# Cluster attention and a softplus feed-forward layer on one core: another table of the issue order behind the first 900 of 3,790 steps, with the engine choices that go with it

## The chip, the cores and the metric

The kernel runs on one core of a Trainium2 chip. The metric is the device time of one execution in microseconds. Its engines are TensorE (PE in the rows; PEld is its weight load), VectorE (DVE), ScalarE (ACT), GpSimd (POOL) and SyncE (SP), which issues the DMAs. Each engine works through its own list in order; an instruction whose input isn't ready holds all that stand behind it on that engine.

## The reference

Four batches of eight heads, 768 positions of 64 elements. Queries and keys are assigned to the nearest of 16 centroids of their head, and a query attends only to keys of its own cluster. The result, as 3,072 rows of 512, goes through two dense layers with a softplus between.

```
q_assign = argmax(q_n . c_n);  k_assign = argmax(k_n . c_n)
scores = q @ k.T / 8, -1e9 where q_assign != k_assign
attn = exp(scores - max) / sum;  x = attn @ v
h = x @ w_in                      # 3072x512 @ 512x2048
g = max(h, 0) + log1p(exp(-|h|))
out = g @ w_out                   # 2048x512
```

## The kernel before, in words

**Attention.** There are 192 tiles, each of 128 queries of one head against that head's 768 keys. For tiles 30 and up `scores` emits four score matmuls (line 1104, 384 columns each), the negated row maximum on VectorE (1120), exp on ScalarE (1131), the cast of the result to an fp16 high part on ScalarE or GpSimd (311, names `phl`), and the low part, a subtraction, on GpSimd or VectorE (1147). A DMA transposition (333, `pt<-phl`) turns both halves, and `attend` multiplies them with the values (1196 to 1198, 18 short matmuls). The scores have two PSUM banks (ring `s`), so a tile's matmuls wait for the exp of the tile two before it.

**First layer.** A pass is 384 tokens of all heads; there are eight. `ffn1` computes a hidden group of 128 columns with twelve matmuls (1275 to 1277), because each fp32 operand is split into two fp16 halves and three of their four products are kept. The hidden groups use two banks (ring `h`). `softplus` follows: exp (1510), log (1511), and a VectorE operation (1526) that frees the bank; then a cast (311, `gh`) and a subtraction (1551). In passes 2 to 6, three of the eight pairs of hidden groups are computed by `seven_of` with seven half-size products in place of eight: three runs of 18, 12 and 12 matmuls (1451 to 1453), with VectorE additions (1462, 1483) and a copy (538) between them. Sums of activations (`tforms`, tile `tf`) and of weights (`wforms`, tiles `wf`, `wg`) are made on VectorE, GpSimd and ScalarE, and the weight sums sit in one buffer each of `pt`, `phl` and `p32` until `give_back`.

**Second layer.** `ffn2` (1895 to 1897, 512 columns) uses one bank (ring `o`); the last two passes use seven products for a whole 2x2 block (1772 to 1774).

**What sets the order.** Every stage is a generator that yields one operation at a time. `Order.run` reads `PLAN`, a string of two-character numbers; each number says which generator emits its next operation. So `PLAN` alone sets the order on all five engines. `either` and `cast` hold two engines for an operation; a key in `SWAPPED` takes the second one. `FILL` puts small matmuls of no use (292) ahead of some of the first matmul operations.

Of the kernel before, what the change touches and what calls it, by code (L numbers as in the profile page):

```python
# [41 lines left out]
SWAPPED = ('S1h_0', 'S1h_2', 'S1l_0', 'S2_2', 'S2_3', 'S2h_2', 'S2h_3', 'S2l_0', 'S2l_2', 'S2l_3', 'S3h_3', 'S3l_1', 'S3l_3', 'S4_0', 'S4_2', 'S4h_0', 'S4h_2', 'S4h_3', 'S4l_0', 'S4l_3', 'T1a_0', 'T1a_1', 'T1a_2', 'T1b_1', 'T1b_2', 'T1h_0', 'T1l_0', 'T1l_2', 'T2a_0', 'T2c_3', 'T2h_0', 'T2h_1', 'T2h_2', 'T2h_3', 'T2l_2', 'T3a_0', 'T3a_1', 'T3a_2', 'T3a_3', 'T3b_1', 'T3c_1', 'T3c_3', 'T3h_0', 'T3h_3', 'T3l_1', 'T4a_0', 'T4a_1', 'T4a_2', 'T4c_0', 'T4c_1', 'T4l_2', 'T4l_3', 'g0_1', 'g0_2', 'g0_4', 'g0_5', 'g0_7', 'g1_1', 'g1_3', 'g1_4', 'g1_6', 'g1_7', 'g2_3', 'g2_7', 'g3_1', 'g3_3', 'g4_0', 'g5_3', 'g5_4', 'g5_5', 'g5_7', 'g6_2', 'g6_3', 'g6_4', 'g6_6', 'g7_4', 'g7_7', 'gh0_0', 'gh0_4', 'gh0_6', 'gh2_2', 'gh2_4', 'gh3_0', 'gh3_1', 'gh3_2', 'gh4_2', 'gh4_4', 'gh4_5', 'gh4_7', 'gh5_1', 'gh5_3', 'gh5_4', 'gh5_6', 'gh6_0', 'gh6_1', 'gh6_2', 'gh6_4', 'gh6_5', 'gh6_6', 'gh6_7', 'gh7_4', 'gh7_5', 'k0_1', 'k10', 'k16', 'k20', 'k24', 'k8', 'kT1_0_1', 'kT1_2_0', 'kh10', 'kh16', 'kh2', 'kh22', 'kh4', 'kh6', 'm0_0_0', 'm0_0_1', 'm0_1_0', 'm20_4_0', 'm20_5_0', 'm28_6_0', 'm4_0_1', 'm8_2_0', 'p108', 'p110', 'p112', 'p114', 'p115', 'p119', 'p121', 'p124', 'p125', 'p127', 'p129', 'p136', 'p137', 'p143', 'p147', 'p151', 'p157', 'p16', 'p161', 'p163', 'p165', 'p169', 'p170', 'p172', 'p173', 'p174', 'p175', 'p176', 'p177', 'p179', 'p18', 'p187', 'p188', 'p189', 'p19', 'p191', 'p21', 'p22', 'p23', 'p26', 'p28', 'p29', 'p32', 'p34', 'p35', 'p37', 'p38', 'p41', 'p46', 'p48', 'p50', 'p51', 'p53', 'p57', 'p59', 'p64', 'p72', 'p75', 'p77', 'p80', 'p81', 'p87', 'p88', 'p93', 'p96', 'p97', 'p98', 'ph103', 'ph104', 'ph105', 'ph106', 'ph107', 'ph108', 'ph110', 'ph111', 'ph112', 'ph113', 'ph114', 'ph115', 'ph117', 'ph120', 'ph125', 'ph130', 'ph132', 'ph133', 'ph135', 'ph137', 'ph140', 'ph141', 'ph153', 'ph154', 'ph155', 'ph156', 'ph159', 'ph163', 'ph164', 'ph165', 'ph177', 'ph179', 'ph181', 'ph187', 'ph191', 'ph20', 'ph30', 'ph36', 'ph45', 'ph48', 'ph53', 'ph59', 'ph68', 'ph72', 'ph78', 'ph86', 'ph89', 'ph90', 'ph93', 'ph95', 'q0_0_0', 'qT0_0', 'qT1_1', 'tf2_1l', 'tf2_2a', 'tf2_2l', 'tf2_3h', 'tf2_4c', 'tf2_4h', 'tf3_1a', 'tf3_1b', 'tf3_1c', 'tf3_1h', 'tf3_1l', 'tf3_2a', 'tf3_2c', 'tf3_3c', 'tf3_3h', 'tf3_3l', 'tf3_4a', 'tf3_4c', 'tf3_4l', 'tf4_1a', 'tf4_2a', 'tf4_2l', 'tf4_3c', 'tf4_3l', 'tf5_1a', 'tf5_1b', 'tf5_1h', 'tf5_1l', 'tf5_2c', 'tf5_3l', 'tf5_4a', 'tf5_4c', 'tf6_1a', 'tf6_1c', 'tf6_1l', 'tf6_2a', 'tf6_2h', 'tf6_2l', 'tf6_3h', 'tf6_3l', 'tf6_4a', 'u10', 'u19', 'u20', 'u21', 'u22', 'u23', 'u27', 'u28', 'u2_3', 'u3_2', 'u3_3', 'u5_4', 'u6_4', 'v0', 'v14', 'v2', 'v2_2', 'v30', 'v3_4', 'v4', 'v5_4', 'v8', 'vh0', 'vh12', 'vh18', 'vh22', 'vh24', 'vh26', 'w17', 'w19', 'w20', 'w21', 'w22', 'w26', 'w27', 'w28', 'w30', 'wb1', 'wb10', 'wb11', 'wb12', 'wb13', 'wb14', 'wb15', 'wb16', 'wb17', 'wb18', 'wb19', 'wb2', 'wb20', 'wb21', 'wb22', 'wb23', 'wb24', 'wb25', 'wb27', 'wb28', 'wb29', 'wb3', 'wb31', 'wb4', 'wb5', 'wb6', 'wb7', 'wb8', 'wb9', 'wf2_1c', 'wf2_1h', 'wf2_2c', 'wf2_2h', 'wf2_2l', 'wf2_3c', 'wf2_3l', 'wf2_4a', 'wf2_4c', 'wf2_4l', 'wf3_1a', 'wf3_1b', 'wf3_1c', 'wf3_1l', 'wf3_2a', 'wf3_2c', 'wf3_3a', 'wf3_3b', 'wf3_3c', 'wf3_4l', 'wf4_1h', 'wf4_1l', 'wf4_2a', 'wf4_2l', 'wf4_3a', 'wf4_3b', 'wf4_3h', 'wf4_3l', 'wh0', 'wh1', 'wh11', 'wh12', 'wh13', 'wh16', 'wh18', 'wh21', 'wh23', 'wh24', 'wh25', 'wh27', 'wh28', 'wh29', 'wh3', 'wh30', 'wh4', 'wh5', 'wh6', 'wk2a', 'wk2b', 'wk2c', 'wk3a', 'wk3b', 'wk3c', 'wk4c', 'x2_0', 'x2_2', 'x3_2', 'x4_1', 'x4_2', 'x5_1', 'x6_1', 'x6_3', 'x7_1', 'xh1_2', 'xh1_3', 'xh2_0', 'xh2_1', 'xh3_0', 'xh3_3', 'xh4_3', 'xh5_2', 'xh6_0', 'xh6_1', 'xh6_3', 'xh7_0', 'xh7_3', 'zk0', 'zk10', 'zk12', 'zk14', 'zk16', 'zk2', 'zk22', 'zk24', 'zk26', 'zk30', 'zk4', 'zk6', 'zk8', 'zq0_0_0', 'zq0_0_1', 'zq12_3', 'zq16_5', 'zq20_5', 'zq24_7', 'zq28_7', 'zq4_0', 'zq4_1', 'zq8_2', 'zq8_3')  # L42
# [25 lines left out]
    "4h0lcz4d4f4f0ld44j4f4agb0ld44h4h4j4h4ld44jgbcz4hcz4l4j4cd44egb4e0o4f4e4l4n0l4nczd44hgcgc4pgc4l0o4e4jgdd44e4l"
    "0pd0cz4ggd4p0o4ncz4ngd4r4p4j4igd4l4rd44tczgd4n4k4t4p0pcz4r4v4pd44rgf4t4rgf0n4nged04p0p4x4vd4gg4t4xd44e4md00p"
    "d00p4v4z4oge4q4td44v4rgegf4zcz4xgf4t4x4q0p4q4v4q0p510pcz4zgf514s4v0p4x534x5153d7d04q554z4z4u51gh53g74w4q5355"  # L70
    "d70p0pghghgh51554zczd7czgi53d7d7gi515557590p57gi4y590p554qcz50d7gi520pd7530p52czgicz59575b52gj5bgj52d05dgk57"
    "0qcz0p5d55d70p54d7d0d7gl575759d74e59d7565bd05fd70q5bgjcz0q5f585d5b5dglgl5h5h595b5d5fczczglgmglgm5h5jgm5fcz5d"
    "5hdagngndadada5f0q5a5c5f525jda5j5h5l5lgn5ed052da5ng95e5j0q5e5lcz5p5h5n5ed0gn5jdacz5lda5l0q5e5g5p5j5i5nda5n0q"
    "gp5rgogngp5ngp5kcz5p5e0q0q0r5r5pcz5l5t5rdagq5n5p0q5t0q5t5m5t525vgqd00r5r0r5egq0qcz5r5vczczczgqda5p0qdade5vgr"
    "gq5o0q5xd0da5z5rd4degr5td4gsgggsd4de0q5x5vde5qdegsd0grgsdegr0rd05vgt0qcz5xd45tdede5xd0615vgs5z5qd40tdedecz0r"
    "d05x0ude61de0r61de5z0tgude5qd063ded0de5zde0r5zguded7d7655q5s5x0r61615ugudfgv65d0dfdf656363630td75q5z5wdf67df"
    "65df63d7df67695y616560670u69d06bd70s690udfgwgwgw62gx62gx676b63cz5q67656dcz0rgxd00r0v69gy676262gxd00v6dgy690s"
    "64gy6b6bgzdg0sgy6b690r0u6fdg6f666ddg6b6d6f6hdg6d68dggy6a6fdgdg6j6h6j6hdgh00rh0h00wd0h16ch1d0h1gxczh26f6hh1cz"
    "0vh2h1h3h3dah362czgv6l6dda6e0u0u0ucz0u6jh40u0r0yh4d00u6hczh40w0udadada0uh4czh60s6l6fh60u6l0w6nd0h60ydhh7dh6p"
    "6ldh6n62dhd06pdh6e6eh46jdh6jd06edh0ydhh8h80zh8h9h96ld0h55q6h6ph96n0w6gh56ncz0w0wczha6ihad06j0w0whbhacz0z0wcz"  # L80
    "cz0w6lha0w6n6phc6phchahc0w6e0zd0czhd6k6mhd0shed0626e0s6n0she6o0she6pgzczh9h90s0scz0z0shf0sd0hf6q0s0s0s0zhf0z"
    "6qd06q0z0x0s6ehe0zczcz0zhe6qhg0z6q6q6q6rdjhidjhi6td06r6rhiczdjdj6r6t6v0z0wdj6rczdj6thi6t6v6v6t6xd0dj6v10hjh7"
    "6x6vdj6z6xdjd06zd06r6t0zhkhj6x6s71d0hj6z0xd0djhidjdj6x716u736vdjdkdj6zdjd06zdk71717371djdjdk7375d06x75730x77"
    "djdkdkdk7775dk796zhm73d077dkhn106whn7b756y7975hnhoho79cz7d117311ho1111hlcz7b71hmd070hphphlhpdldlhpdld00zdldl"
    "d0hpdldldlhqhrhohrhrhsd0hshs117d1111cz7779hs77cz75791172d0hqhsho11ht0x72htht117bdm111111dm11d01172dm77dm727d"
    "74dmdmdmdm7d11hu767bhuhuhvhvhvd00x7bcz7978hw0x7d0x0xhv0x0x7b0x0xcz0x0xhx0x7dhxhx0xd07a72hxcz10hxhvczcz72czhy"
    "hyhy7f7hcz7c7f7f7f7h7h727h7jhz7fcz7l7j7l7h7f7ed07j7j7h7e7n7e7li07l7e7pd07j7j7ehz7e7n7nd07g7p7l7i7rhz7pi07n7p"
# [1896 lines left out]
```

## Time and profile before

| | us |
|---|---|
| timed runs: median of 3 | 852.97 |
| lowest and highest | 846.71, 854.46 |
| the profiled execution | 853.94 |
| its span in the trace | 852.2 |
| busy: TensorE, VectorE, ScalarE, GpSimd | 789.3, 693.8, 523.0, 598.4 |

The span runs from the first instruction to the last, and the profiled execution's own time is 1.7 us more. A busy engine is one with an instruction in flight. TensorE's matmuls overlap, and their ends are modelled: a 384-column matmul is shown as 0.33 us long, though the next one starts 0.16 us after it. So a gap between two matmuls that the trace calls idle is shorter than the time by which the second is late.

### The profile page before, as it was taken

The numbers are of one execution on the slowest core, as the hardware profiler recorded it, in microseconds if no ns is written. First come the engines' busy times: TensorE is split into PE (matmuls) and PEld (weight loads), VectorE is DVE, ScalarE is ACT, GpSimd is POOL, SyncE is SP. The second block draws the span as 40 slices with busy tenths as digits, with TensorE's granted clock in tenths as the row PEclk, the third lists the DMA queues.
The fourth block names the chain that finished last, engine by engine and source line by source line (L and its number), as shares of the span: only waits on it lengthen the run. The fifth ranks groups of instructions, "written<-read, shape, count | busy, mean of one in ns | idle before, by whom it ended". The sixth has DMA issues, their size and how long they took to land. (4 is left out here: it accounts for less than half of the span.)

```text
span 852.2 us, 20795 instructions
## 1 busy us (share of the span) xinstructions
PE 789.3 (93%) x8374; PEld 540.3 (63%) x8374; DVE 693.8 (81%) x1131; ACT 523.0 (61%) x846; POOL 598.4 (70%) x498
## 2 busy tenths in 40 slices
...
GB/s 311 242 254 157 101 189 250 204 209 205 199 197 196 186 154 184 141 181 105 154 121 196 189 197 169 201 182 166 141 157 184 155 136 94 59 113 23 33 1 56
DMA packets 402420, 136.15 MB, mean 160 GB/s; under 512 B 379028, under 2 KB 395924, under 8 KB 402324
## 3 DMA queue, kind: packets, MB, share of 16 engines
...
q14 instruction: 31, 0.25, 0.1%
...
## 5 line engine op out<-in xcount | busy, mean ns | idle before, releaser
L1147 POOL TENSOR_TENSOR phl<-p,phl 128x768 f16<-128x768 f32 x104 | 179.9, 1733 | 54.9 <-ACT phl L311 49.6
L1131 ACT ACTIVATE p<-s,negm 128x768 f32<-128x768 f32 x162 | 144.8, 896 | 86.9 <-DVE negm L1120 72.7
L1120 DVE TENSOR_REDUCE negm<-s 128x1 f32<-128x768 f32 x162 | 151.8, 948 | 16.3 <-PE s L1104 16.2
L1104 PE MATMUL s<-kt,qt 128*128 128x384 f16 x648 | 130.3, 325 | 8.8 <-ACT p L1131 6.5
L1275 PE MATMUL h<-xT,wi 128*128 128x384 f16 x392 | 128.4, 328 | 8.1 <-DVE fg L1526 6.0
L1276 PE MATMUL h<-xT,wi 128*128 128x384 f16 x392 | 128.4, 327 | 0.0
L1277 PE MATMUL h<-xT,wi 128*128 128x384 f16 x392 | 128.3, 327 | 0.0
L1196 PE MATMUL mbank<-vb,pt 128*128 128x65 f16 x1056 | 111.7, 192 | 7.6 <-DMA pt<-phl 5.1
L1198 PE MATMUL mbank<-vb,pt 128*128 128x65 f16 x1056 | 111.3, 194 | 0.9 <-DVE pt L1071 0.9
L1197 PE MATMUL mbank<-vb,pt 128*128 128x64 f16 x1056 | 111.6, 192 | 0.0
L1895 PE MATMUL o<-wo,gh 128*128 128x512 f16 x288 | 109.0, 379 | 2.3 <-DVE ot L1918 1.6
L1896 PE MATMUL o<-wo,gh 128*128 128x512 f16 x288 | 109.1, 379 | 0.1
L1897 PE MATMUL o<-wo,gh 128*128 128x512 f16 x288 | 109.1, 379 | 0.0
L1196 PEld LDWEIGHTS <-pt 128*128 128x128 f16 x1056 | 97.6, 98 | 18.0 <-DMA pt<-phl 9.0
L311 ACT CAST phl<-p 128x768 f16<-128x768 f32 x113 | 93.3, 829 | 25.3 <-DMA pt<-phl 20.7
L1197 PEld LDWEIGHTS <-pt 128*128 128x128 f16 x1056 | 97.2, 97 | 11.2 <-issue 2.7
L1198 PEld LDWEIGHTS <-pt 128*128 128x128 f16 x1056 | 97.3, 97 | 1.0 <-DVE pt L1071 1.0
L1510 ACT ACTIVATE fa<-h 128x384 f32<-128x384 f32 x98 | 47.8, 489 | 78.7 <-PE h L1277 74.6
L1104 PEld LDWEIGHTS <-qt 128*128 128x128 f16 x648 | 59.7, 97 | 49.0 <-issue 10.7
L1147 DVE TENSOR_TENSOR phl<-p,phl 128x768 f16<-128x768 f32 x58 | 67.8, 1171 | 7.4 <-POOL phl L311 4.0
L311 POOL CAST phl<-p 128x768 f16<-128x768 f32 x49 | 44.4, 909 | 28.7 <-ACT p L1131 17.7
L1511 ACT ACTIVATE fa<-fa 128x384 f32<-128x384 f32 x113 | 59.0, 523 | 2.3
...
## 6 DMA issues: line engine op xcount, KB each, us to landing
...
pt<-phl SPq DMA_TRANSPOSE x162, 4.0
...
```

What stands on the lines that cost most here:

```text
L311: (e.copy if e is nc.scalar else e.tensor_copy)(dst, src)
L1104: nc.tensor.matmul(st[:, j, :SH], qt[:, s, i], kt[:, s, NT // 2 * j : NT // 2 * (j + 1)], start=(s == 0), stop=(s == 1),)
L1120: yield op("DVE", 950, lambda: nc.vector.tensor_reduce(negm, st[:, :, :SH], AX.XY, ALU.max, negate=True))
L1131: yield op("ACT", 900, lambda: nc.scalar.activation(p32, st[:, :, :SH], AF.Exp, bias=negm, scale=size))
L1147: lambda e: e.tensor_tensor(phl[:, 1], p32, phl[:, 0], ALU.subtract),
L1196: nc.tensor.matmul(av, pt[:, 0, c], vb[:, c, D : 2 * D + 1], start=(c == 0), stop=False)
L1197: nc.tensor.matmul(av[:, :D], pt[:, 0, c], vb[:, c, :D], start=False, stop=False)
L1198: nc.tensor.matmul(av, pt[:, 1, c], vb[:, c, D : 2 * D + 1], start=False, stop=(c == NT - 1))
L1275: nc.tensor.matmul(hp, w[0], x[0], start=(c == 0), stop=False)
L1276: nc.tensor.matmul(hp, w[0], x[1], start=False, stop=False)
L1277: nc.tensor.matmul(hp, w[1], x[0], start=False, stop=(c == NP - 1))
L1896: nc.tensor.matmul(po, g[0], wo[:, f, 0, 1], start=False, stop=False)
```

## The change

Three tables of numbers change, and nothing else: `FILL`, `SWAPPED` and `PLAN`. `PLAN` keeps its first 900 entries and its length of 3,790. `SWAPPED` goes from 451 to 474 keys, of which 290 are the same. On GpSimd there are 22 more instructions, on ScalarE 17 fewer, on VectorE 5 fewer; TensorE has two more of the filling matmuls and otherwise the same ones; SyncE issues the same DMAs. TensorE's list is the same up to its first output matmul of tile `o_0_2_0` (at 170.2 us in the trace of before) and again in its last 295 matmuls (from 816.6 us).

```
-FILL = {0: 40, 3: 8, 5: 12, 8: 11, 12: 6, 15: 10, 16: 7, 19: 30, 22: 7, 25: 3, 28: 5}
+FILL = {0: 40, 3: 8, 5: 12, 8: 11, 12: 7, 15: 10, 16: 10, 19: 28, 22: 7, 25: 3, 28: 5}
...
-    "3mcz0g3xd03tcz0ifx41cwfxfw3xcz0g3xfxczfy0gfy3o3q0k0k3vfxd0fzd03q0kfud0cwg1fz3qcxcwfz3zcw410kcwcxcz0ncz3zg0g3"
+    "3mcz0g3xd03tcz0ifx41cwfxfw3xcz0g3xfxczfy0gfy3o3q0k0k3vfxd0fzd03q0kfud0cwcx0k0kg1fzcwcwfzczcw3qcxg03z0n3qcz0k"
...
```

Three places show what moves. The first is VectorE around the row maxima of head 10 of the 32 (counted from 0 over all batches), tiles 0 to 2 (`negm_10_1` is the one of tile 1); `phl` rows of line 1147 are low parts, `wf_2` a weight sum, `aq`, `eq_q` and `n2` the cluster assignment of later queries, `fg` softplus. Before:

```order
L892 TENSOR_SCALAR n2_110<-eq_q12_2_3308 128x12x16
L1147 TENSOR_TENSOR phl_112<-p32_9_2_3385,phl_112 128x768
L1628 TENSOR_TENSOR wf_2_3400<-wi_121 128x256 x2
L972 TENSOR_TENSOR eq_q12_2_3308<-eq_q12_2_3308,al_12_2952 128x192
L973 TENSOR_REDUCE aq_12_2_3426<-eq_q12_2_3308 128x12
L1526 SCALAR_TENSOR_TENSOR fg_1_0_3383<-fa_1_1_3401,h_1_1_3350 128x384
L1120 TENSOR_REDUCE negm_10_1_3461<-s_10_1_3392 128x1
L1120 TENSOR_REDUCE negm_10_2_3479<-s_10_2_3471 128x1
```

Now:

```order
L1120 TENSOR_REDUCE negm_10_0_3409<-s_10_0_3394 128x1
L972 TENSOR_TENSOR eq_q12_2_3293<-eq_q12_2_3293,al_12_2987 128x192
L1628 TENSOR_TENSOR wf_2_3416<-wi_121 128x256
L973 TENSOR_REDUCE aq_12_2_3370<-eq_q12_2_3293 128x12
L1120 TENSOR_REDUCE negm_10_1_3433<-s_10_1_3408 128x1
L1526 SCALAR_TENSOR_TENSOR fg_1_0_3399<-fa_1_1_3417,h_1_1_3342 128x384
L1628 TENSOR_TENSOR wf_2_3416<-wi_121 128x256
L1147 TENSOR_TENSOR phl_112<-p32_10_0_3428,phl_112 128x768
L1120 TENSOR_REDUCE negm_10_2_3485<-s_10_2_3435 128x1
```

The maximum of tile 1 stood behind a subtraction, two weight sums and a softplus operation; now one weight sum and the two small operations stand between it and the maximum before it, and the rest comes after it.

The second is TensorE in pass 3, where `seven_of` goes from its second run to its third in the bank `h_3_5` (weights `wi`, then the weight sum in `pt`). Before:

```order
L1453 LDWEIGHTS wi_121
L1453 MATMUL h_3_5_6212<-xT_4_6063,wi_121 128x192
L1451 LDWEIGHTS pt_113
L1451 MATMUL h_3_5_6212<-xT_3_4707,pt_113 128x192
L1452 LDWEIGHTS pt_113
```

Now:

```order
L1453 LDWEIGHTS wi_121
L1453 MATMUL h_3_5_6173<-xT_4_6067,wi_121 128x192
L1196 LDWEIGHTS pt_113
L1196 MATMUL mbank_119<-vb0_102,pt_113 128x65
L1197 LDWEIGHTS pt_113
L1197 MATMUL mbank_119<-vb0_102,pt_113 128x64
```

The third run followed at once; now two tiles' attention and a tile's scores stand between.

The third is GpSimd at tiles 14_4 to 15_4 of pass 3 (tiles 4 of head 14 to 4 of head 15, counted as above; names `phl<-p32_14_4` and so on; `kn`, `vb` and `gh` are the splits of keys, values and softplus results). Before:

```order
L1147 TENSOR_TENSOR phl_112<-p32_14_4_5396,phl_112 128x768
L311 CAST wi_121<-wg_4_5463 128x2x128
L1628 TENSOR_TENSOR wi_121<-wg_4_5463,wi_121 128x2x128
L311 CAST phl_112<-p32_15_3_5581 128x768
L1232 TENSOR_TENSOR xn_1_3_5220<-x32_11_3_5218,xn_1_3_5220 128x2x3x64
L1551 TENSOR_TENSOR gh_2_1_5562<-fg_2_1_5471,gh_2_1_5562 128x768
L1147 TENSOR_TENSOR phl_112<-p32_14_5_5454,phl_112 128x768
```

Now:

```order
L311 CAST phl_112<-p32_14_4_5429 128x768
L689 TENSOR_TENSOR kn1_20_5414<-rawk_20_5379,kn1_20_5414 128x12x64
L1628 TENSOR_TENSOR wi_121<-wg_4_5398,wi_121 128x2x128
L1147 TENSOR_TENSOR phl_112<-p32_14_4_5429,phl_112 128x768
L1147 TENSOR_TENSOR phl_112<-p32_14_5_5516,phl_112 128x768
L311 CAST gh_2_1_5529<-fg_2_1_5454 128x768
L311 CAST phl_112<-p32_15_3_5587 128x768
L1551 TENSOR_TENSOR gh_2_1_5529<-fg_2_1_5454,gh_2_1_5529 128x768
L526 TENSOR_TENSOR vb1_104<-rawv_18_5194,vb1_104 128x12x64
L311 CAST phl_112<-p32_15_4_5629 128x768
L1147 TENSOR_TENSOR phl_112<-p32_15_4_5629,phl_112 128x768
L1147 TENSOR_TENSOR phl_112<-p32_15_3_5587,phl_112 128x768
```

The low part of tile 15_3, which was on VectorE, is now on GpSimd, behind eleven others in this piece, that of the later tile 15_4 among them.

## Rows read from the trace of the kernel before

**Rows 1.** Windows by stage: us, busy time of each engine (instructions), granted clock, DMA.

```profile
core 0: us, PE busy (x) PEld busy (x) DVE busy (x) ACT busy (x) POOL busy (x), PEclk, DMA share, GB/s
170.00:816.00 646.00, 606.62 (x6217) 394.75 (x6217) 511.45 (x822) 378.87 (x602) 460.01 (x372) 1.00 0.83 153
...
sum 852.20, PE 789.26 PEld 540.27 DVE 693.76 ACT 523.02 POOL 598.44; mean PE 263.09 PEld 180.09 DVE 231.25 ACT 174.34 POOL 199.48
```

**Rows 2.** Waits, 170 to 816 us: who waited for whom, us, times, longest.

```profile
PE s L1104 <- ACT p L1131: 6.5, 10, 1.5
PE h L1451 <- DVE fw L1462: 5.8, 6, 1.7
PE mbank L1196 <- DMA pt<-phl: 5.1, 6, 1.6
PE h L1451 <- DVE fg L1526: 4.8, 4, 1.8
...
PE cnt L759 <- DVE fg L1526: 2.0, 2, 1.8
...
PE o L1895 <- DVE ot L1918: 1.6, 2, 1.0
```

**Rows 3.** Timeline of TensorE, 205 to 210 us: start, us, line, shape, idle before.

```profile
205.53 0.33 PE L1275 MATMUL h<-xT,wi 128*128 128x384 f16 x1
205.69 0.33 PE L1276 MATMUL h<-xT,wi 128*128 128x384 f16 x1
...
209.41 0.81 PE L1104 MATMUL s<-kt,qt 128*128 128x384 f16 x4 [1.55 <-ACT p L1131]
```

**Rows 4.** Timelines of VectorE and ScalarE in the same stretch.

```profile
204.88 0.96 DVE L1147 TENSOR_TENSOR phl<-p,phl 128x768 f16<-128x768 f32 x1 [0.71 <-POOL phl L311]
...
206.95 0.54 DVE L1526 SCALAR_TENSOR_TENSOR fg<-fa,h 128x384 f32<-128x384 f32 x1
207.41 1.81 DVE L1120 TENSOR_REDUCE negm<-s 128x1 f32<-128x768 f32 x2
...
208.46 0.90 ACT L1131 ACTIVATE p<-s,negm 128x768 f32<-128x768 f32 x1 [2.32 <-DVE negm L1120]
```

**Rows 5.** Timeline, 392 to 400 us: from the second run to the third.

```profile
395.18 0.25 PE L1453 MATMUL h<-xT,wi 128*128 128x192 f16 x1
...
395.46 0.56 DVE L1462 TENSOR_TENSOR fw<-h,fe 128x384 f32<-128x384 f32 x1 [0.67 <-PE h L1453]
...
396.07 0.24 PE L1451 MATMUL h<-xT,pt 128*128 128x192 f16 x1 [0.65 <-DVE fw L1462]
```

**Rows 6.** The page's DMA issues: count, us from issue to landing.

```profile
pt<-phl SPq DMA_TRANSPOSE x162, 4.0
```

**Rows 7.** Line 1196, matmuls and weight loads: idle before it until, us, times.

```profile
  DMA pt<-phl: 14.1, 18
```

**Rows 8.** Groups by form on ScalarE and VectorE: count, busy us, mean ns, idle before.

```profile
L1510 ACT ACTIVATE fa<-h 128x384 f32<-128x384 f32 x98 | 47.8, 489 | 78.7 <-PE h L1277 74.6 <-DVE kb L1526 1.9 <-DVE fg L1526 1.1
L1511 ACT ACTIVATE fa<-fa 128x384 f32<-128x384 f32 x113 | 59.0, 523 | 2.3
...
L1526 DVE SCALAR_TENSOR_TENSOR fg<-fa,h 128x384 f32<-128x384 f32 x80 | 43.4, 547 | 16.3 <-ACT fa L1511 12.9 <-POOL gh L1551 1.7 <-issue 0.6
```

**Rows 9.** Groups by form on GpSimd.

```profile
L1147 POOL TENSOR_TENSOR phl<-p,phl 128x768 f16<-128x768 f32 x104 | 179.9, 1733 | 54.9 <-ACT phl L311 49.6 <-issue 1.2 <-DVE negm L1120 1.2
L1551 POOL TENSOR_TENSOR gh<-fg,gh 128x768 f16<-128x768 f32 x31 | 55.8, 1803 | 2.5 <-ACT gh L311 2.1
L311 POOL CAST phl<-p 128x768 f16<-128x768 f32 x49 | 44.4, 909 | 28.7 <-ACT p L1131 17.7 <-DMA pt<-phl 6.9 <-DVE n L892 2.4
...
L526 POOL TENSOR_TENSOR vb<-rawv,vb 128x768 f16<-128x768 f32 x10 | 17.0, 1698 | 0.1
```

**Rows 10.** The stage 700 to 750 us, in the columns of the first group.

```profile
700.00:750.00 50.00, 43.23 (x425) 28.21 (x424) 37.43 (x57) 27.09 (x45) 35.62 (x31) 1.00 0.45 86
```

**Rows 11.** Line 1147 on VectorE: count, ns least/median/most, first and last start.

```profile
L1147 DVE TENSOR_TENSOR phl<-p,phl x58: 942/959/2441, 117.7 to 757.8; 128x768 f16<-128x768 f32 x58
```

More of the change, by code (lines that the diff above doesn't have):

```diff
@@ L68 @@
[L68 to L87, printed above, removed]
@@ new lines @@
+    "4h0p4g4rgcd44j4p4id4d44ncz0ogd4p4t4r4n0p4lg74pcz4k4n0pgfcz4rczd44p4v4r4e4t4p4r4tgfd4ge4m0p4rd04v4x0ngg0p4tgf"
+    "4vgg4vgd0ocz4o4x4zczgd4qgg4t4xgh4zgg4e4t4v4x4x0p4vd04qd70pd74qgggh514z4qd0514s4zgh4ugh51cz0pd7d74q0p4z53cz53"
+    "5151554e4xcz0p4q53gi4wcz4z4yd755d7gid753550pgj0p575955gi50d70p51gi53gi575957cz5557d70p0p4q5252czgj59d05b5d53"
+    "57d70q550pgld759d70pd0d7gj595b5752gk525dd054cz5bcz5f0qgk0qgkgm5d5bgk5d5b5f565f59cz5h5h525d5b58gm5fgkcz5j5hd0"
+    "0q5f5agngm5j5l5ddadadagn5c5j5f5h5n52gng9cz0q5l5hcz5nda0qda5eda5j5j0q0qgo5e5e5e5lgnd0go5lda5n0q5pgn5ego0r5g5p"
@@ new lines @@
+    "cz5ldacz5h5r5pcz5ndacz5jgq0q5lgq0r5p0q5i5rgpda5n525n5egq5tdagq5p0rdad05tgr5kczda5egeczgq0qde5r5r0qd0gs5t5m5v"
+    "gs5xded05rde0qd05v5xde5p5odegr0qgs5rded45t5tgr5vd4gs5qdegtgrde5x5vcz5q0qd4d4d00rde5xde5zgsd05z5v5t5zded4de5x"
+    "61de61de0r5zczde5vgu63gu5qde0r0rd00td0610rdegugv61d761de650u0r5z5q0tdf635s63dfdf0u5x5udf5wdf65670rdf65d7d05z"
+    "0r63d7610tdf675qdf635yd7gwd0czgwd7650s6769gwgxcz6763gx69650u6b0s5q6062gxd06269gy676dgy6bgx6965d0626bgy676dgy"
+    "dg626b6f0vdg6469dg0ugz6f6ddgdg666b68gydggxdgd06bdgd0h0h00s6hcz0rczdah06h696fda0w6d0rh1h2h1h1h16jh26d0ud062h3"
```

80 lines of the change are left out of this document (45 added, 35 removed).

## The prediction, made before the changed kernel ran

> **What bounds the kernel now.** I read the windows by stage first. The order differs only from 170 to 816 us, and there TensorE is busy for 606.6 of 646 us, at a granted clock of 1.00; VectorE has 511.5, GpSimd 460.0 and ScalarE 378.9 us [rows 1]. No other engine is near its limit over the stretch, and the change leaves TensorE's matmuls as they are. So what another order can win or lose lies in the 646 - 606.6 = 39.4 us in which TensorE has nothing in flight. It is a little more by starts: successive 384-column matmuls start 0.16 us apart and are shown 0.33 us long [rows 3], so each wait is about 0.17 us longer than the idle shown.
>
> The waits come next [rows 2]. No single one is large: the longest is 2.0 us, and the four largest groups, 22.2 us together, are 26 waits with four causes. Scores wait for the exp that frees their bank; a run of `seven_of` waits for the addition before it, or for a softplus; attention waits for its transposition. The reader is to see that the lost time is spread thin, over engines that are each late now and then.
>
> Third, two places in detail. At 209.41 TensorE waits 1.55 us for an exp [rows 3]. That exp started at 208.46, after 2.32 us in which ScalarE waited for row maxima, and these started on VectorE at 207.41, right behind a softplus operation that began at 206.95 in a queue that begins with a subtraction at 204.88 [rows 4]. The scores were ready long before: it is a place in VectorE's queue. From 395.18 to 396.07 the third run of `seven_of` waits for an addition that begins 0.28 us after the last matmul of the second run began and takes 0.56 us [rows 5]: here nothing stands between the two runs, and the chain itself is the wait.
>
> **The change part by part.** TensorE's two more filling matmuls stand in the first 25 us, where it waits anyway: nothing. GpSimd takes 22 more instructions, mostly casts of 0.9 us and some low parts of 1.7 us [rows 9], some 18 us by form; ScalarE has some 13 us less and VectorE 2 less. All three have idle time in the stretch, 186, 267 and 134 us [rows 1], so as sums these cost nothing. If that cover is gone somewhere, GpSimd's excess falls on low parts, transpositions and attention; that is the slower rival. The rest is order, and I cost it by counting, in both orders, the places of the kinds that wait in the trace. A distance below is the matmul work between two places on TensorE, counted with start-to-start times like those of rows 3.
>
> 1. *Scores soon after the tile two before.* Less than 2.5 us of matmuls between: 9 tiles before, 2 now. The nine hold about 4.0 of the group's 6.5 us [rows 2], the wait of rows 3 among them; its maximum is also moved ahead in VectorE's list. 7/9 of 4.0 is -3.1 us. Ends: nothing, and -6.5.
> 2. *Runs of `seven_of` close together.* Six distances of at most 0.65 us before, six now. But both of the second-to-third changes with nothing between (about 0.8 us each, as in rows 5) go, and one of that kind comes. The other five of now are first-to-second changes; at 0.65 us one of that kind had no wait in the trace, and one of now has nothing between, which I take at 0.5 us by the same chain less the longer addition. The sum goes from 2.4 to 1.3: -1.1. Ends: 0, and -5.8, the whole group [rows 2].
> 3. *Attention soon after its transposition.* The transposition lands 4.0 us after its issue [rows 6]. Emitted with less than 4 us of matmuls to go: 65 tiles before, 50 now. Matmuls waited 5.1 us for these [rows 2], with the weight loads 14.1 us [rows 7], and part of the loads' wait lies under running matmuls. 15/65 of these are -1.2 and -3.3; I take -2.5, since a late load does make its matmul late.
> 4. *Output groups close together.* Under 1.5 us between: 8 before, 5 now; 3/8 of 1.6 us [rows 2] is -0.6. Ends: 0 and -1.6.
> 5. *Hidden groups soon after the one two before.* Under 2 us between: none before, 5 now (1.57 to 1.94). Exp, log and the freeing operation take 0.489 + 0.523 + 0.547 = 1.56 us without a queue [rows 8]. I take 0.2 us each, +1.0; with one row maximum ahead of them on VectorE (two take 1.81 us [rows 4]) it would be 0.9 each, +4.5. Low end nothing.
> 6. *A first run right behind a softplus that frees its bank.* 8 before, 13 now; 4.8/8 = 0.6 us each [rows 2]: +3.0. Ends: 0 and +3.0.
> 7. *Cluster counts (line 759) right behind a softplus.* 4 before, 6 now; 2.0/4 each [rows 2]: +1.0.
>
> The sum is -3.1 - 1.1 - 2.5 - 0.6 + 1.0 + 3.0 + 1.0 = -2.3 us. The profiled execution took 853.9 us (its span of 852.2 [rows 1] and 1.7 around it), 1.0 above the median of 852.97. Against it the change gives 851.6; on the scale of the median 850.7, so I say **851 us**. With the gains in full and no losses it is -7.3, 846; with half the gains and losses at their upper ends (4.5 + 3.0 + 1.0 - 3.7) it is +4.8, 858.
>
> What stays, and why I expect little: most of the 39.4 us is not at short distances. Of the waits before a run of `seven_of`, the longest come with plenty of matmuls between and a VectorE queue that is late, and another order of the same work makes other queues late. Late next, where 209.41 is mended, is the maximum of tile 2: a softplus, a weight sum and a low part now stand between the two maxima, some 2 us, and only where the scores after it come later than that is the wait gone rather than moved.
>
> **The rivals.** *Faster: the crowded places thin out too.* The gains 1 to 4 come in full and the losses 5 to 7 don't (the hidden groups' 1.56 us fits the distances if no queue is late). And the stage with the most idle time, 700 to 750 us, with 6.8 us [rows 10] against 3.0 for a mean 50 us of the stretch, comes down to that mean: VectorE's work emitted in the 50 us of matmuls there falls from 48.6 to 43.1 us. That is -7.3 - 3.8 = -11.1: 842 us. For it: the closest distances of scores and of runs did get rarer. Against it: places where a DVE, ACT or GpSimd instruction stands directly before the matmul that needs it number 153 before and 155 now.
>
> *Slower: GpSimd becomes late in places.* In no 25 us of matmul work before does GpSimd's list hold over 25 us of work; now three do, with 28.4, 27.8 and 27.1, 8.3 over. For VectorE the excess over matmul work rises from 18.8 to 24.1. One place shows the mechanism: up to the low part of tile 15_3 GpSimd has, from the low part of 14_3 on, five subtractions of 1.73, six casts of 0.91, two splits of 1.70 and one of 1.80 us, 19.3 us [rows 9]; with the 4.0 of its transposition [rows 6] that is 23.3, against some 20.4 us of matmuls up to its attention, with 39.4/606.6 of waits added 21.7. Attention would wait 1.6 us there. It decides once such an excess passes the waits that are there anyway. If all of it reaches TensorE, 8.3 + 5.3 - 2.3 = +11.3: 864 us. Against it: before, an excess of 18.8 us on VectorE did not show as a wait of that size at any one place.
>
> *Slower by the port.* A low part on VectorE takes 0.942 at least, 0.959 in the median and 2.441 us at most [rows 11]: few are stretched, and the worst by 1.5 us, near a whole subtraction of 1.73 on GpSimd [rows 9]. If each microsecond that GpSimd gains held VectorE up and all of that reached TensorE, it would be 18 - 2.3 = +15.7: 869 us. By the median's closeness to the least it is next to nothing, and VectorE's 134 idle us [rows 1] cover it. The Trainium skill speaks for this rival: its page "SBUF — State Buffer", section "SBUF: two separate sides", says that VectorE and GpSimd share one pair of ports under an exclusive lock, and the loser stands still for the whole instruction. By that rule, the trace's longest duration agrees, and more two-input work on GpSimd would be paid for on VectorE; by the rows the sum stays as it is.
>
> **How the numbers follow.** Chances: the forecast 46 in 100, the faster rival 32, GpSimd late 17, the port 5. About 1% is what a measurement here can tell from no change: the three runs before span 0.9%. So faster by over 1% (below 844.4) has 0.32, within 1% 0.46, slower (above 861.5) 0.22. The forecast's own range is 846 to 858. The range for 8 in 10 reaches from 839, 3 us below the faster rival's value, to 864, which takes in the late GpSimd but not the port.
>
> **What would show it.** Right: TensorE idle from 170 to 816 us between 33 and 44 us, waits of scores for exps below 4 us, of runs for softplus up by 2 or 3, no wait at `h_3_5`'s third run, and about as many waits as now. The faster rival: idle below 30 us, and 700 to 750 no worse than its neighbours. GpSimd late: attention waiting for transpositions over 20 us in all, with GpSimd busy without a gap before 15_3. The port: the median of line 1147 on VectorE well above 0.96 us. I would be wrong altogether if TensorE's own matmul time changed, or if the difference came before 170 or behind 816 us, where the order is the same.

## The result, and the profile after

The changed kernel took 825.64 us in the median of four runs (822.31 to 828.05), against 853.72 for the kernel before on the same chip: a ratio of 0.968, with a 95% interval of 0.962 to 0.975. That is 28 us less where 2 were forecast, and below the range. The direction is that of the faster rival, the size 2.5 times its 11 us. The profiled execution took 825.76 us.

The windows by stage (answering [rows 1]; TensorE's stretch with the changed order now ends at 788 us), then the stage of [rows 10]:

```profile
170.00:788.00 618.00, 601.78 (x6175) 392.97 (x6171) 514.66 (x812) 367.40 (x582) 481.41 (x392) 0.99 0.88 159
...
sum 824.00, PE 786.02 PEld 540.65 DVE 695.17 ACT 513.22 POOL 624.69; mean PE 262.01 PEld 180.22 DVE 231.72 ACT 171.07 POOL 208.23
...
700.00:750.00 50.00, 49.98 (x493) 35.23 (x492) 42.52 (x56) 26.07 (x45) 45.79 (x38) 1.00 0.49 96
```

TensorE's idle time in the stretch went from 39.4 to 618 - 601.8 = 16.2 us. Counted by starts (a matmul is late by how much more than its usual distance it starts after the one before), all matmuls of the kernel together are some 81 us late before and some 53 now, with the same work: the 28 us between them are the whole difference. The stage 700 to 750 has no gap left; by the clock it holds later work than before, but the work that stood there now runs from 680 to 722 us, without a gap either and in 42 us for 50. The waits of TensorE in the stretch, with the columns of [rows 2]:

```profile
PE mbank L1196 <- DMA pt<-phl: 6.3, 7, 2.5
PE s L1104 <- DMA qt<-n: 3.3, 4, 1.7
PE o L1895 <- DVE ot L1913: 2.0, 1, 2.0
PE s L1104 <- ACT p L1131: 1.1, 1, 1.1
PE h L1451 <- DVE fw L1462: 0.7, 1, 0.7
PE h L1451 <- DVE fg L1526: 0.6, 1, 0.6
```

Of the six kinds in [rows 2] one grew (attention for its transposition) and five almost went. What is left is mostly DMA.

Where it came from: the scores of tile 91 can be found in every trace. In the profiled executions they start at (timeline of TensorE, before and after, and the windows up to there):

```profile
321.05 0.81 PE L1104 MATMUL s<-kt,qt 128*128 128x384 f16 x4
0.00:321.04 321.04, 293.18 (x3402) 206.84 (x3403) 283.67 (x495) 243.85 (x398) 225.03 (x207) 0.99 0.97 204
```

```profile
324.39 0.81 PE L1104 MATMUL s<-kt,qt 128*128 128x384 f16 x4
0.00:324.38 324.38, 299.45 (x3458) 211.65 (x3459) 290.50 (x506) 241.50 (x397) 230.19 (x209) 0.99 0.97 203
```

Behind it, before needs 852.2 - 321.0 = 531.1 us and the change 824.0 - 324.4 = 499.6. But the two orders don't have the same work ahead of it: 3,402 matmuls stood ahead of these scores, and 3,458 do now. Of the 56 between them two are filling, and 54 (12 of output groups, 24 half-size ones, 18 of attention) stood behind tile 91 before; at the start-to-start distances of the timelines (0.216, 0.082 and 0.03 us) these take 5.1 us. So of the 31.5 us 5.1 are work that is moved ahead and 26.4 are won; up to tile 91 some 2 us are won. The scores of tile 146 halve the rest: 253.6 and 277.5 us became 238.1 and 261.4. This split of each profiled execution is used below beside the times. Before, e2, e5, e6, e9, e11 and e13 to e15 have the 54 matmuls behind tile 91, all others ahead of it, so runs of one kind compare directly. Behind tile 91 the split is sharp: executions with the changed kernel's lists there took 499.6, 499.9 and 501.1 us, two with those of before 531.1 and (without the 54 matmuls) 527.8. Up to tile 91 it isn't: before, e9 and e13 to e15, which are the same there, took 316.2 to 322.6 us, kernels with the lists of after 317.3 to 329.7.

| run | median us | ratio to before, 95% | to tile 91 | 91 to 146 | 146 to end |
|---|---|---|---|---|---|
| before | 853.7 to 856.5 | 1 | 321.0 | 253.6 | 277.5 |
| after | 825.6 | 0.962 to 0.975 | 324.4 | 238.1 | 261.4 |
| e1 order of after, engines of before | 900.4 | 1.049 to 1.061 | 342.2 | 261.1 | 295.2 |
| e2 order of before, engines of after | 931.3 | 1.082 to 1.098 | 341.8 | 282.1 | 304.1 |
| e3 after up to tile 91, then before | 855.3 | 0.994 to 1.002 | 324.6 | 250.0 | 277.8 |
| e4 before up to tile 91, then after | 828.7 | 0.966 to 0.977 | 326.7 | 237.8 | 262.1 |
| e5 before, 35 late producers ahead | 860.8 | 1.003 to 1.011 | 318.6 | 255.8 | 283.3 |
| e6 before, 35 at random ahead | 877.3 | 1.023 to 1.037 | 319.9 | 265.5 | 290.7 |
| e7 after, 18 late producers ahead | 828.0 | 0.963 to 0.977 | 327.8 | 238.0 | 264.3 |
| e8 after from tile 91 to 146 only | 839.3 | 0.976 to 0.990 | 326.2 | 236.8 | 276.6 |
| e9 before, half row maximum | 844.4 | 0.984 to 0.992 | 316.2 | 254.3 | 274.8 |
| e10 after, half row maximum | 826.5 | 0.963 to 0.971 | 326.0 | 237.6 | 261.2 |
| e11 before, 26 of the 35 | 852.1 | 0.993 to 0.999 | 314.6 | 257.3 | 274.0 |
| e12 after, 15 of the 18 | 824.4 | 0.962 to 0.971 | 329.7 | 238.8 | 261.7 |
| e13 before, half exp | 855.2 | 0.994 to 1.002 | 322.6 | 251.6 | 280.0 |
| e14 before, half split on GpSimd | 849.6 | 0.989 to 0.997 | 316.6 | 249.4 | 274.1 |
| e15 before, all three halved | 843.4 | 0.977 to 0.992 | 321.7 | 249.7 | 270.9 |
| e16 after, all three halved | 822.1 | 0.955 to 0.968 | 329.7 | 235.7 | 258.1 |
| e17 after, 35 at random ahead | 844.5 | 0.982 to 0.993 | 329.7 | 249.1 | 267.7 |
| e18 after, filling of before | 827.9 | 0.961 to 0.975 | 317.3 | 237.6 | 263.5 |

Three executions of e3 and one of e5 were in a slower state, and the ratios leave them out; without them the medians are 852.6 and 860.0 us.

### The profile page after: what moved, and what is told of

Its sections match the earlier page's. It is cut to its first block, busy times and chain, and to the rows that moved or that the text cites. A ratio compares the mean times of both kernels' runs of the same rounds, so it can differ in the third digit from the quotient of the medians.

```text
span 824.0 us, 20807 instructions
## 1 busy us (share of the span) xinstructions
PE 786.0 (95%) x8376; PEld 540.7 (66%) x8376; DVE 695.2 (84%) x1126; ACT 513.2 (62%) x829; POOL 624.7 (76%) x520
## 4 chain that ended last, share of the span: by engine, by line
PE 49%; DMA 15%; DVE 14%; POOL 9%; issue 7%; ACT 5%; SPq 1%; POOLq 0%; DVEq 0%; ACTq 0%
DMA pt<-phl 9%; PE s L1104 7%; PE h L1275 5%; PE h L1276 4%; PE h L1277 4%; PE o L1895 4%; PE o L1896 4%; PE o L1897 4%; POOL phl L1147 3%; DMA qt<-n 2%; PE m L1773 2%; PE m L1774 2%; PE m L1772 2%; PE mbank L1196 2%; PE mbank L1198 2%
## 5 line engine op out<-in xcount | busy, mean ns | idle before, releaser
L1147 POOL TENSOR_TENSOR phl<-p,phl 128x768 f16<-128x768 f32 x98 | 169.6, 1736 | 31.4 <-ACT phl L311 27.6
L1197 PEld LDWEIGHTS <-pt 128*128 128x128 f16 x1056 | 97.2, 97 | 10.2 <-issue 1.9
L311 ACT CAST phl<-p 128x768 f16<-128x768 f32 x106 | 87.7, 829 | 22.8 <-DMA pt<-phl 18.4
L311 POOL CAST phl<-p 128x768 f16<-128x768 f32 x56 | 57.8, 1031 | 33.8 <-ACT p L1131 21.6
L1147 DVE TENSOR_TENSOR phl<-p,phl 128x768 f16<-128x768 f32 x64 | 73.0, 1141 | 5.3 <-ACT phl L311 3.7
```

Of the source, the lines that this page charges most:

```text
L311: (e.copy if e is nc.scalar else e.tensor_copy)(dst, src)
L1147: lambda e: e.tensor_tensor(phl[:, 1], p32, phl[:, 0], ALU.subtract),
L1197: nc.tensor.matmul(av[:, :D], pt[:, 0, c], vb[:, c, :D], start=False, stop=False)
```

## The experiments

**Order or engines: e1 and e2.** The change has three parts, the order (`PLAN`), the engines (`SWAPPED`; 345 of 1,096 choices differ) and the filling matmuls. Each of the first two alone, e1 as an edit of the changed kernel, e2 the reverse in the one before:

```diff
-SWAPPED = ('E1_1', 'S1h_0', 'S1h_1', 'S1l_1', ...
+SWAPPED = ('S1h_0', 'S1h_2', 'S1l_0', 'S2_2', ...
```

> The table of the issue order is that of the change, the engine choices are those of before. If the gain of 28 us lies in the order (theory ORDER), most of it stays: 824 to 834 us. If it lies in which engine does what (ENGINES): 848 to 858. If the two are fitted to each other (FIT), an operation on the other engine takes another time and stands in the wrong place of its list, and nothing is kept: 850 or more, perhaps above before.

> The other way round: the order of before with the engine choices of the change. ORDER: no gain, 848 to 858. ENGINES: 824 to 834. FIT: no gain or a loss, 850 to 870.

Both lose, 45 and 76 us: neither part has a gain of its own, as FIT had it, though e2 came out far beyond FIT's 850 to 870. In e2 the waits of TensorE grow in the kinds of [rows 2], and for hidden groups (line 1275, 6.0 us in the whole of before); the whole execution:

```profile
PE s L1104 <- ACT p L1131: 21.6, 24, 2.7
PE h L1451 <- DVE fg L1526: 11.5, 5, 4.2
PE h L1275 <- DVE fg L1526: 11.1, 10, 2.2
PE h L1451 <- DVE fw L1462: 8.2, 7, 3.0
```

An order fits one set of durations and queues; a third of the engine choices exchanged makes it a bad order.

**Where: e3, e4 and e8.** Order and engines of one kernel up to the scores of a tile, and of the other behind. The rows of `PLAN` change from there on (e3 as an edit of the changed kernel, e4 and e8 of the one before; e8 changes back at tile 146):

```diff
-    "dg626b6f0vdg6469dg0ugz6f6ddgdg666b68gydggxdgd06bdgd0h0h00s6hcz0...
+    "dg626b6f0vdg6469dg0ugz6f6ddgdg666b68gydggxdgd06bdgd0h0h00s0v696...
```

```diff
-    "64gy6b6bgzdg0sgy6b690r0u6fdg6f666ddg6b6d6f6hdg6d68dggy6a6fdgdg6...
+    "64gy6b6bgzdg0sgy6b690r0u6fdg6f666ddg6b6d6fdgdg68gydggxdgd0dgd0h...
```

> Order and engine choices of the change up to the scores of tile 91 (about 325 us), then those of before for all that is left. At that place the two traces are within 2 us of each other. If the gain is made behind it, 850 to 856; if the first stretch prepares it (work done earlier that the later stages live on), 826 to 845.

> The order and choices of before up to the scores of tile 91, then those of the change. If the gain is made behind it, all of it comes: 824 to 829. If the first stretch prepares it: 835 to 855.

> Order and engines of the kernel before up to the scores of tile 91 (some 325 us), of the changed kernel from there to those of tile 146 (some 535 us), and of the kernel before again behind them. LOCAL (each stretch's gain is its own): the gain that the changed kernel has made between these two matmuls, 13 us, so 838 to 845 us. SYSTEMIC (the gain needs the whole order behind): 850 us or more.

The lists behind tile 91 alone win 26 us (e4), those ahead of it nothing (e3). In e8 the middle stretch takes the 237 us that it takes in the changed kernel, and the rest the 277 that it takes in the kernel before. The gain is local and adds up; no stretch prepares another. (As said, e4 and e8 run the 54 matmuls ahead of tile 91, as the changed kernel does.)

**Can the late places be mended one by one? e5 and e6, e7, e11 and e12.** 32 of the 43 us that matmuls start late behind 285 us in the kernel before stood behind a producer whose inputs were there before it began. So e5 moves 35 such instructions ahead by 1 to 4 places; one of them on VectorE, from the timeline at 606 us:

```diff
 L642 TENSOR_TENSOR eq_q<-sim_q,mx_q
+L1526 SCALAR_TENSOR_TENSOR fg<-fa,h
 L648 TENSOR_TENSOR eq_q<-eq_q,tab
 L650 TENSOR_REDUCE best_q<-eq_q
 L652 TENSOR_TENSOR eq_q<-eq_q,best_q
 L892 TENSOR_SCALAR n<-eq_q
-L1526 SCALAR_TENSOR_TENSOR fg<-fa,h
 L972 TENSOR_TENSOR eq_q<-eq_q,al
```

> The order of the kernel before, with 35 instructions (24 on VectorE, 10 on ScalarE, 1 on GpSimd) moved ahead by 1 to 4 places in their own engine's list; TensorE's list, the engines and all the rest stay. Each of them released a late matmul behind 285 us, and its inputs had been there before it began. The places cover 32 of the 43 us that matmuls start late behind 285 us. QUEUE PLACES (late time is where a producer stands in its list, and each place can be mended by itself): at least half of the 32 us go, 822 to 840 us. CONSERVED (the sentence of the prediction: another order of the same work makes other queues late): 846 to 860 us. FRAGILE (any change of the lists off a searched order costs, as exchanged engines did): over 862 us.

The control moves as many others by the same distances; one on ScalarE, at 398 us:

```diff
 L311 CAST phl<-p
+L1510 ACTIVATE fw<-h
 L1131 ACTIVATE p<-s,negm
 L1131 ACTIVATE p<-s,negm
-L1510 ACTIVATE fw<-h
```

> Control for the run above: as many instructions on the same engines, by the same distances, but drawn at random between 285 and 790 us. QUEUE PLACES: most have time to spare, nothing much happens, 852 to 860 us. CONSERVED: 850 to 858 us. FRAGILE: over 865 us.

The mends win nothing: +6 us, at the far end of CONSERVED. The control costs 22 us, some 0.6 us for each instruction moved. Its trace shows how. ScalarE and TensorE in e6 at the place above:

```profile
392.71 0.83 ACT L311 CAST phl<-p 128x768 f16<-128x768 f32 x1
397.35 0.49 ACT L1510 ACTIVATE fw<-h 128x384 f32<-128x384 f32 x1 [3.81 <-DVE fe L1483]
397.74 1.68 ACT L1131 ACTIVATE p<-s,negm 128x768 f32<-128x768 f32 x2
...
398.68 0.81 PE L1104 MATMUL s<-kt,qt 128*128 128x384 f16 x4 [2.35 <-ACT p L1131]
```

and ScalarE in the kernel before:

```profile
394.35 0.90 ACT L1131 ACTIVATE p<-s,negm 128x768 f32<-128x768 f32 x1
397.00 0.90 ACT L1131 ACTIVATE p<-s,negm 128x768 f32<-128x768 f32 x1 [1.76 <-DVE negm L1120]
398.25 0.49 ACT L1510 ACTIVATE fw<-h 128x384 f32<-128x384 f32 x1 [0.34 <-DVE fe L1483]
```

The moved instruction reaches the head of ScalarE's list before its input exists and idles the engine for 3.81 us; the exp behind it, which ran at 394.35 before, runs at 397.74, and TensorE waits 2.35 us for the bank. Too early in a list is as bad as too late.

In e5 the example shows the other way in which a mend is lost. VectorE there, GpSimd beside it and TensorE behind:

```profile
606.78 0.54 DVE L1526 SCALAR_TENSOR_TENSOR fg<-fa,h 128x384 f32<-128x384 f32 x1
...
608.31 0.82 DVE L892 TENSOR_SCALAR n<-eq_q 128x192 f16<-128x192 f16 x1
609.16 1.68 DVE L972 TENSOR_TENSOR eq_q<-eq_q,al 128x192 f16<-128x192 f16 x1
...
613.08 0.68 DVE L1918 SCALAR_TENSOR_TENSOR ot<-o,ot 128x512 f32<-128x512 f32 x1
```

```profile
608.20 0.83 POOL L311 CAST phl<-p 128x768 f16<-128x768 f32 x1 [2.42 <-ACT p L1131]
608.99 1.64 POOL L1147 TENSOR_TENSOR phl<-p,phl 128x768 f16<-128x768 f32 x1
```

```profile
613.81 0.38 PE L1895 MATMUL o<-wo,gh 128*128 128x512 f16 x1 [2.69 <-DVE ot L1918]
```

VectorE before:

```profile
608.32 0.23 DVE L892 TENSOR_SCALAR n<-eq_q 128x192 f16<-128x192 f16 x1
608.45 0.55 DVE L1526 SCALAR_TENSOR_TENSOR fg<-fa,h 128x384 f32<-128x384 f32 x1
608.91 0.67 DVE L972 TENSOR_TENSOR eq_q<-eq_q,al 128x192 f16<-128x192 f16 x1
...
611.83 0.68 DVE L1918 SCALAR_TENSOR_TENSOR ot<-o,ot 128x512 f32<-128x512 f32 x1
```

and TensorE before:

```profile
612.61 0.38 PE L1895 MATMUL o<-wo,gh 128*128 128x512 f16 x1
```

The softplus operation comes 1.67 us sooner, and the run behind it too. But line 892 now starts beside a cast on GpSimd and takes 0.82 us for 0.23, and line 972 beside a low part and takes 1.68 for 0.67; each ends within 0.25 us of the GpSimd instruction. The output's addition then starts 1.25 us later, while TensorE gets there 1.7 us earlier, and waits 2.69 us where it had not waited. Even durations hang on who stands beside whom.

The loss of e5 as a whole is in good part the clock. Its windows and TensorE's timeline behind the wait of 2.69 us:

```profile
614.30:617.70 3.40, 3.40 (x17) 2.22 (x16) 2.58 (x3) 0.00 (x0) 1.22 (x2) 0.50 1.10 205
638.20:641.60 3.40, 3.31 (x32) 2.99 (x32) 1.92 (x4) 0.90 (x1) 0.57 (x1) 0.50 0.62 116
658.70:662.10 3.40, 2.87 (x25) 1.86 (x25) 3.40 (x4) 2.79 (x5) 1.74 (x1) 0.50 1.20 211
```

```profile
615.02 0.63 PE L1896 MATMUL o<-wo,gh 128*128 128x512 f16 x1
615.44 0.63 PE L1897 MATMUL o<-wo,gh 128*128 128x512 f16 x1
```

The granted clock is 0.50 there, 1.2 GHz in place of 2.4, and matmuls of 512 columns start 0.42 us apart, not 0.22. The other two stretches stand at waits of 2.39 and 2.08 us. At half the clock the three cost some 5 us (an estimate, half their length) of the 8.0 that e5 is slower behind tile 91; the kernel before has no such stretch between there and its last matmul. Without them e5 would still be some 3 us slower there. In the ten executions of e5 the granted clock was 0.986 to 0.994, in those of the kernel before beside them 0.994 to 0.999.

Then 18 such mends in the changed kernel (e7), and second passes in which the moves that had made a neighbour late are taken back, 9 of e5's (e11; the one shown among them) and 3 of e7's (e12):

```diff
-L1526 SCALAR_TENSOR_TENSOR fg<-fa,h
 L648 TENSOR_TENSOR eq_q<-eq_q,tab
 L650 TENSOR_REDUCE best_q<-eq_q
 L652 TENSOR_TENSOR eq_q<-eq_q,best_q
 L892 TENSOR_SCALAR n<-eq_q
+L1526 SCALAR_TENSOR_TENSOR fg<-fa,h
```

> The changed kernel with 18 producers moved ahead in the same way (13 on VectorE, 4 on ScalarE, 1 on GpSimd); their places cover some 10 of the 16 us that matmuls start late behind 285 us. QUEUE PLACES: 815 to 821 us, faster than the changed kernel. CONSERVED: 823 to 828. FRAGILE: over 830.

> Second pass over the 35 moves of the run that came out at 861 us: 9 of them are taken back, since within 4 us behind each another instruction of the same list, displaced by it, became late by 0.8 to 3.4 us (15 us in all, against some 5 us that these 9 had won). 26 moves stay. QUEUE PLACES (late places can be mended one at a time if the displaced one has time): 843 to 851 us. CONSERVED (what a mend wins, the next late place takes): 852 to 860 us.

> The same second pass over the 18 moves in the changed kernel: 3 are taken back, which had cost 4.6 us in all. QUEUE PLACES: 819 to 824 us, faster than the changed kernel. CONSERVED: 825 to 828 us.

None of them wins anything behind tile 91 that can be told. e11 came out at 852.1, at the near end of CONSERVED. Its interval, 0.993 to 0.999, lies just below 1, but behind tile 91 it took 531.3 us, as the kernel before did; e7 took 828.0, and e12 824.4, between the two expectations, with 500.5 us behind tile 91. No version that beats the changed kernel came of it.

**Is it backlog? e9, e10, e13 to e16.** If producers are late because too much work stands ahead of them, less work must help. From tile 91 on, one half of a row is left out: in VectorE's maximum (e9, e10), ScalarE's exp (e13), the casts and low parts of the probabilities on GpSimd (e14), or all three (e15, e16):

```diff
-        yield op("DVE", 950, lambda: nc.vector.tensor_reduce(negm, st[:, :, :SH], AX.XY, ALU.max, negate=True))
+        row = st[:, :1, :SH] if t >= 91 else st[:, :, :SH]
+        yield op("DVE", 950, lambda: nc.vector.tensor_reduce(negm, row, AX.XY, ALU.max, negate=True))
```

```diff
-        yield op("ACT", 900, lambda: nc.scalar.activation(p32, st[:, :, :SH], AF.Exp, bias=negm, scale=size))
+        h = 1 if t >= 91 else 2
+        yield op("ACT", 900, lambda: nc.scalar.activation(p32[:, :h], st[:, :h, :SH], AF.Exp, bias=negm, scale=size))
```

```diff
-            lambda e: e.tensor_tensor(phl[:, 1], p32, phl[:, 0], ALU.subtract),
+            lambda e: (lambda k: e.tensor_tensor(phl[:, 1, :k], p32[:, :k], phl[:, 0, :k], ALU.subtract))(
+                g if e is nc.gpsimd else 2
+            ),
```

> The kernel before; from the scores of tile 91 on (some 325 us) the row maximum on VectorE reads one half of the row, 384 of 768 elements (the second half is left out of the maximum). All lists and engines stay; VectorE gets some 0.4 us less in each of 85 tiles, about 34 us, and the chain from scores to exp is as much shorter. PACED (the late time behind 325 us is backlog: the producers stand behind real work in VectorE's list, and the changed kernel's gain is that its list has less of it in the wrong place): 830 to 844 us. INTRINSIC (the late time is set by the order of the lists, whatever the work in them): 848 to 856 us.

> The same edit in the changed kernel. PACED: little backlog is left to take away, so 3 to 8 us less, 818 to 823 us, and the two orders come closer, their distance falls from 28 us to under 20. INTRINSIC: less than 3 us, and the distance stays at 25 us or more.

> The kernel before; from tile 91 on ScalarE's exp of the scores takes one half of the row (384 of 768 elements; the other half is read as a repeat of the first), lists and engines as they were. BACKLOG EVERYWHERE (what the halved row maximum left of the late time lies behind work in the other engines' lists): 843 to 850 us. INTRINSIC: 852 to 857 us.

> The kernel before; from tile 91 on the casts and low parts of the probabilities that GpSimd makes cover one half of the row (the other half keeps what an earlier tile left), lists and engines as they were. It also halves the subtractions that could hold VectorE up at the port they share. BACKLOG EVERYWHERE: 842 to 850 us. INTRINSIC: 852 to 857 us.

> Row maximum, exp and GpSimd's casts and low parts halved together from tile 91 on, in the kernel before. BACKLOG EVERYWHERE: the order of before is no longer worse than that of the changed kernel, 820 to 830 us. INTRINSIC: the halved row maximum's 844 us and little more, 838 to 846 us.

> The same three halvings in the changed kernel. BACKLOG EVERYWHERE: 815 to 822 us, within 10 us of the order of before with the same edit. INTRINSIC: 820 to 826 us, 15 us or more below the order of before with the same edit.

By its time e9 won 11 us, just short of PACED. The split of its profiled execution shows less: behind tile 91, where alone it differs, it took 529.1 us, 2.0 less than before, and 4.9 of the profiled difference lie ahead of it. That execution, 847.1 us, was the second longest of six; the shortest, 839.7, can't have taken over some 523 us behind tile 91 unless its first stretch was shorter than the 314.6 us that is the least of all. So what the halved maximum wins lies between 2 and 11 us, and how much isn't settled. With it the orders are 18 us apart by their times (e9, e10), which PACED had, and 30.3 behind tile 91, which INTRINSIC had. With all three halved the old order still takes 520.6 us there and the new one 493.8: less the 5.1 of moved work, 21.7 of the 26.4 us between the orders stay, and 21 of 28 by the times. e15 and e16 came out as INTRINSIC had it: the pair that was to show the distance closing shows it open. e13 agrees, and e10 by its own time. Only e14 came out as backlog had it, and GpSimd's half is the largest share behind tile 91 (7.6 us of the 10.5 of e15); so some 10 us of the old order's time there is backlog or port; most of the distance isn't. TensorE's waits in e15, 325 to 790 us:

```profile
PE mbank L1207 <- DMA pt<-phl: 4.5, 6, 1.5
PE h L1462 <- DVE fw L1473: 3.8, 4, 1.5
PE sim_k L618 <- DMA kt<-kn: 2.2, 2, 1.8
PE s L1104 <- ACT p L1133: 1.8, 3, 1.0
```

Scores wait for exps for 1.8 us (4.0 in this stretch before), their own chain being shorter; the runs of `seven_of` (line 1451 is 1462 here), the transposed keys and attention wait where they did. Most of the distance between the orders comes from where things stand, not from how much of this work there is.

**More time to spare, or a better fit? e17 and e18.** The control of e6 in the changed kernel (moves of the kind shown there), and the filling matmuls alone:

```diff
-FILL = {0: 40, 3: 8, 5: 12, 8: 11, 12: 7, 15: 10, 16: 10, 19: 28, 22: 7, 25: 3, 28: 5}
+FILL = {0: 40, 3: 8, 5: 12, 8: 11, 12: 6, 15: 10, 16: 7, 19: 30, 22: 7, 25: 3, 28: 5}
```

> The changed kernel with 35 instructions drawn at random between 285 and 765 us moved ahead in their lists, with the numbers per engine and the distances of the same control in the order of before (which cost 22 us there). MARGINS (the new order is better because its producers have more time to spare): 10 us or less, up to 836 us. FITTED (each list is fitted to the others, and a displacement costs the same in any fitted order): 840 to 852 us.

> The changed kernel with the filling matmuls of the kernel before (two fewer, in the first 25 us). If these play no part: 824 to 828 us. If the clock or the start hangs on them: over 830 us.

35 random displacements cost the new order 19 us, the old one 22 (one draw each): FITTED. The new lists are no more forgiving, and most of their gain goes with 35 of the 2,475 instructions of the three engines 1 to 4 places further ahead. The filling has no share.

## Why the prediction was wrong

**The failed step** is "What stays, and why I expect little: most of the 39.4 us is not at short distances", with its reason that "another order of the same work makes other queues late". The reason holds for an edit of a finished order: e5, e11 and e12 won nothing that can be told behind tile 91. It doesn't hold between two orders that are each fitted as a whole: the new one has less lateness of nearly all kinds, 16.2 us of idle time for 39.4. I costed the change like an edit. Its marks that I had named came true for the faster rival: less than 30 us of idle time, and a stage from 700 to 750 us no worse than its neighbours.

- *Scores after exps* (-3.1, end -6.5): 6.5 to 1.1 us, -5.4, near its far end. The place of [rows 3, 4] mended as described. The maximum of tile 1 now starts at 203.92, ahead of the softplus operation, the weight sum and the low part, and that of tile 2 at 207.11, behind them. The scores at 207.73, which had waited, and the next ones at 209.90 both start without a wait, so the wait is gone and not moved. VectorE's and TensorE's timelines of after:

```profile
203.92 0.96 DVE L1120 TENSOR_REDUCE negm<-s 128x1 f32<-128x768 f32 x1 [0.41 <-PE s L1104]
...
206.24 0.95 DVE L1147 TENSOR_TENSOR phl<-p,phl 128x768 f16<-128x768 f32 x1
207.11 0.94 DVE L1120 TENSOR_REDUCE negm<-s 128x1 f32<-128x768 f32 x1
```

```profile
207.73 0.81 PE L1104 MATMUL s<-kt,qt 128*128 128x384 f16 x4
...
209.90 0.81 PE L1104 MATMUL s<-kt,qt 128*128 128x384 f16 x4
```

- *Runs of `seven_of` close together* (-1.1, end -5.8): 5.8 to 0.7, so -5.1. As many distances are short as before; the long ones stopped being late too. The third run of [rows 5] starts right behind other matmuls at 389.16, its addition done at 388.65 (TensorE and VectorE of after):

```profile
388.51 0.81 PE L1104 MATMUL s<-kt,qt 128*128 128x384 f16 x4
389.16 0.25 PE L1451 MATMUL h<-xT,pt 128*128 128x192 f16 x1
```

```profile
388.10 0.55 DVE L1462 TENSOR_TENSOR fw<-h,fe 128x384 f32<-128x384 f32 x1
```

- *First runs and cluster counts right behind a softplus* (+3.0 and +1.0): wrong in sign. 4.8 fell to 0.6 us and 2.0 to nothing, although more places stand directly behind one. Standing next in the lists isn't being late: what counts is how long the producer had been done, and no count of places tells that.
- *Attention after its transposition* (-2.5): wrong in sign, 5.1 to 6.3 us, and 14.1 to 17.0 with the weight loads [rows 2, 7]; the transposition still takes 4.0 us from issue to landing.
- *Output groups* (-0.6): line 1918's 1.6 us went, and waits at line 1913 grew from 0.5 to 2.0 us. *Hidden groups* (+1.0): waits of line 1275 for softplus sum to 0.3 us in the stretch. Both small, as said.
- *Not costed at all*: attention waiting for the scaled result that frees its bank (line 1220, 2.3 us) and cluster similarities waiting for the transposed keys (333, 2.1) or for line 1526 (1.9) had some 6 us of single waits before, and have 0.3.
- *The sums of the engines* (nothing): held, though GpSimd's busy time in the whole kernel rose by 26.3 us, not by the 18 reckoned from the forms. It works 481.4 us in a stretch 28 us shorter and isn't late. At the place named for tile 15_3 it is busy without a gap, as forecast, up to the end of the low part at 348.24 (GpSimd, and the transposition behind it):

```profile
344.09 0.82 POOL L311 CAST phl<-p 128x768 f16<-128x768 f32 x1
344.99 3.25 POOL L1147 TENSOR_TENSOR phl<-p,phl 128x768 f16<-128x768 f32 x2
```

```profile
348.27 4.27 SPq L333 DMA_TRANSPOSE pt<-phl  x2
```

  But the attention of these two tiles runs at 354.27 and 354.82 without a wait: a full queue for 25 us didn't make a matmul late where it was placed for that.
- *The port*: its sign was to be line 1147's median on VectorE well above 0.96 us [rows 11]. It is 0.958:

```profile
L1147 DVE TENSOR_TENSOR phl<-p,phl x64: 942/958/2126, 116.0 to 726.7; 128x768 f16<-128x768 f32 x64
```

  Its mean fell from 1,171 to 1,141 ns. So the port had no share in these as a sum; e5 shows it at work in single places.

In numbers: idle time fell by 23.2 us in the stretch where 2.3 were forecast. The two softplus terms, forecast as losses, are 10.2 us off, scores and runs, which were too small, 6.3, the kinds left out some 6, and attention 3.7 the other way; with hidden groups (1.0) and single waits of less than 1 us each that makes up the miss. What stays open is what makes the new lists better, in a number that could be read off them beforehand. The runs show that it isn't the counts of near places, the engines' sums or, for the larger part, the amount of the work that was halved. They don't tell TensorE's own list from the lists of the other engines: no run gives TensorE the one order and the other engines the other.
